# First-layer weights loaded by row blocks, six accumulators, and GpSimd normalizing the repeated rests: one change at the head of a fused attention and MLP kernel

## The chip, the cores and the metric

The kernel runs on one core of one Trainium2 chip. The metric is the device time of one execution in microseconds (us), median of several runs. Each number in a profile is from one profiled execution; its own device time stands beside its span below, since the span runs only from the first to the last instruction.

## The reference

For 2048 tokens of width 448, with xn the layer-normalized x:

```python
xn  = (x - mean(x)) / sqrt(var(x) + 1e-5)
q, k, v = split(xn @ wqkv, heads=16, width=28)
phi(t)  = where(t > 0, t + 1, exp(t)) + 1e-6
kv  = sum_s phi(k)[s] v[s]^T ;  z = sum_s phi(k)[s]
s   = (phi(q) @ kv / (phi(q) . z + 1e-6)) @ wo
h   = relu(xn @ w1 + b1) ** 2            # w1: 448 x 1792
g   = silu(h @ w2 + b2)                  # w2: 1792 x 448
out = x + s * g
```

All inputs and the output are bf16. Only the way from x and w1 to the first columns of h is touched by the change.

## The kernel before

**Tiles.** Tokens go in 16 tiles of 128 (index `si`), or in 4 groups of 512 (`g`). The contraction over 448 is cut into three chunks of 128 rows (c = 0, 1, 2) and a rest of 64 rows (c = 3). A rest would fill only half of TensorE's rows, so xn keeps its last 64 columns twice (columns 384 to 447 and again at 448 to 511), its transpose `xT` holds the rest in partitions 0 to 63 and again in 64 to 127, and two tiles' rests are run side by side in the two halves. The 1792 columns of h are 14 tiles (`fi`); `w_1` holds chunks 0 to 2, `w_1r` the rests.

**Order.** Every operation is recorded by `add` (L61) with its engine, the data it reads and writes and a guessed duration. `schedule` (L89) keeps PE (TensorE) and SP (the DMA issuing queue) in the order written, orders ACT (ScalarE), DVE (VectorE) and POOL (GpSimd) by readiness and due time, and hands out the eight PSUM banks. `emit` (L240) adds semaphore waits. At the head of the kernel `pr.hot` (L1202 to L1237) fixes the order on the three other engines as written, too.

**Loads at the head.** SP issues, in this order: x of token tiles 0, 1, 2 and 3 (L443 to L445); w1 in column blocks p of 512 columns (`load_w1`, L429): of p = 0 chunk 0 (128 KB), then chunks 1 and 2 (256 KB); of p = 1 all three chunks (384 KB) and two rest pieces of 32 KB; then x of tiles 4 to 7 (448 KB) and the k part of wqkv. ACT issues b1 and the two rest pieces of p = 0. Later, when the first transposed chunk of tokens 2 and 3 exists, SP issues w1 for p = 2 (384 KB and two rests), the q part of wqkv, then w1 for p = 3 (192 KB and two rests), and x of tiles 8 to 11. All issues are at L400.

**The first tokens.** For tiles 0 to 3: statistics on DVE (L463, L465), 1/std on ACT (L472, L476), xn on DVE (L483), the repeat of the rest by a copy (`dup`, L723: POOL for tiles 0, 1, 2, DVE for tile 3), transposes on PE (L743) and their copies from PSUM into `xT` (`evac`, L758 on DVE, L759 on ACT), one per chunk for tiles 0 and 1. Then h of group 0, in halves of 256 tokens: `pe_part` (L709) runs column tiles 0 to 3 for the first half chunk by chunk (12 matmuls), then tiles 4 and 5 with all three chunks (6 matmuls); 8 transposes of tiles 2 and 3; tile 6 (3 matmuls); the second half of tiles 0 to 3 (12 matmuls), their rests (L713, 4 matmuls), the second half of 4 to 6 (9), tile 7 (3), and the rests of 4 to 7 (4). Each finished column tile is relu'd (L680 on ACT, L685 on DVE) and squared (L694, L695), and its bank comes free.

**What follows.** Quads of k tiles and h tiles alternate (L1257). The first, K0.0 H0.8 K0.1 H0.10, needs the k weights, the p = 2 columns of w1 with both rests, and the banks of the first four column tiles (K0.0 and K0.1 those of tiles 0 and 2, H0.8 and H0.10 those of 1 and 3). Tokens from 512 on are transposed by DMA (L497), issued by SP behind the loads.

Of the kernel before, what the change touches and what calls it, by code (L numbers as in the profile page):

```python
# [6 lines left out]
ALU = mybir.AluOpType  # L7
AF = mybir.ActivationFunctionType

P = 128  # L10
S, D, F = 2048, 448, 1792
# [34 lines left out]
class Program:  # L46
# [14 lines left out]
    def add(self, eng, emit, reads=(), writes=(), dur=0.2, alts=(), nbytes=0):  # L61
        reads = [p for r in reads for p in self.aliases.get(r, (r,))]
        op = Op(eng, emit, reads, writes, dur, alts, nbytes)
        op.lead = self.lead
        if self.hot is not None:
            self.hot += 0.01
            op.prio = op.rank = self.hot
        for t in op.reads:
            w = self.writer.get(t)
            if w is not None:  # L70
                op.raw.add(w)
            self.readers.setdefault(t, []).append(op)
        for t in op.writes:
            w = self.writer.get(t)
            if w is not None and w is not op:
                op.deps.add(w)
            for r in self.readers.get(t, ()):
                if r is not op:
                    op.deps.add(r)
            self.writer[t] = op  # L80
            self.readers[t] = [r for r in self.readers.get(t, ()) if r is op]
        op.raw.discard(op)
        op.deps |= op.raw
        for d in op.deps:
            d.succ.append(op)
        self.ops.append(op)
        return op
# [212 lines left out]
def bass_recurrent_scan__linear_attn_block__dense_activation_squared_relu__prompt_kernel(  # L300
    nc, A_x, A_wqkv, A_wo, B_x, B_w1, B_b1, B_w2, B_b2, out
):
    with ExitStack() as es:
# [5 lines left out]
        ident = sb("ident", [P, P], bf)  # L309
# [5 lines left out]
        x_tok = sb("x_tok", [P, NT, D], bf)  # L315
        wqh = sb("wqh", [P, 64], bf)
        xn = sb("xn", [P, NT, 512], bf)
        xT = sb("xT", [P, NT, 4, P], bf)
        w_qkv = sb("w_qkv", [P, 4, 3 * D], bf)
        w_1 = sb("w_1", [P, 3, F], bf)  # L320
        w_1r = sb("w_1r", [P, 896], bf)
# [6 lines left out]
        mv = sb("mv", [P, NT, 2], f32)  # L328
        vep = sb("vep", [P, NT], f32)
        rstd = sb("rstd", [P, NT], f32)  # L330
# [68 lines left out]
        def dma(eng, dst, src, writes, nbytes, reads=(), dur=0.6):  # L399
            op = add(eng, lambda e, _: e.dma_start(dst, src), reads, writes, dur, nbytes=nbytes)  # L400
            if eng == "act":
                op.prio = -1000.0 + len(pr.ops)
# [4 lines left out]
        def load_w1r(p, eng2):  # L407
            lo, hi = 512 * p, min(512 * p + 512, F)
            m = (hi - lo) // 2
            for i in (0, 1):  # L410
                dma(
                    eng2, w_1r[64 * i : 64 * i + 64, 256 * p : 256 * p + m],
                    B_w1[384:448, lo + m * i : lo + m * i + m], [("w1", p, 1 + i)], 128 * m,
                )
# [11 lines left out]
        half_of = lambda fi: 1 if fi % 4 >= 2 or fi == 13 else 0  # L426
        rest_col = lambda fi: 768 if fi >= 12 else (fi // 4) * 256 + (fi % 2) * P

        def load_w1(p, eng, eng2, reads=()):  # L429
            lo, hi = 512 * p, min(512 * p + 512, F)  # L430
            m = (hi - lo) // 2
            for c0, c1 in ((0, 1), (1, 3)) if p == 0 else ((0, 3),):
                dma(
                    eng, w_1[:, c0:c1, lo:hi], B_w1[c0 * P : c1 * P, lo:hi].rearrange("(c p) j -> p c j", p=P),
                    [("w1", p, 0, c) for c in range(c0, c1)], (c1 - c0) * 256 * (hi - lo), reads,
                )
            load_w1r(p, eng2)

        w1names = lambda p: [("w1", p, i) for i in range(3)]
        for p in range(4):  # L440
# [3 lines left out]
        load_x(1, 2)  # L444
        load_x(2, 4)  # L445
        dma("act", b1r[:, :], B_b1.rearrange("(f p) -> f p", p=P), ["b1r"], F * 2)
        load_w1(0, "sp", "act")
        load_w1(1, "sp", "sp")
        load_x(4, 8)
        load_k("sp", w_qkv, A_wqkv, "wk", D, 2 * D)  # L450

# [15 lines left out]
        def ln_rstd(lo, hi):  # L467
            c = slice(lo, hi)
            ts = range(lo, hi)
            add(  # L470
                "act",
                lambda e, _: e.activation(out=vep[:, c], in_=mv[:, c, 1], func=AF.Ln, bias=eps5[:, 0:1]),  # L472
                [("mv", i) for i in ts] + ["eps5", "actw"], [("vep", i) for i in ts], 0.25,
            )
            add(
                "act", lambda e, _: e.activation(out=rstd[:, c], in_=vep[:, c], func=AF.Exp, scale=-0.5),  # L476
                [("vep", i) for i in ts], [("rstd", i) for i in ts], 0.2,
            )

        def ln_norm(si):  # L480
            add(
                "dve",
                lambda e, _: e.tensor_scalar(  # L483
                    out=xn[:, si, 0:D], in0=x_tok[:, si, :], scalar1=mv[:, si, 0:1],
                    scalar2=rstd[:, si : si + 1], op0=ALU.subtract, op1=ALU.mult,
                ),
                [("x", si), ("mv", si), ("rstd", si)], [("xn", si)], 0.36,
            )
# [81 lines left out]
        def pe_part(us, part, cs=(0, 1, 2)):  # L570
            def f(e, _):
                last = None
                for k in cs:
                    for u in us:
                        last = u[2](e, slice(0, 128), k, k == 0, False, part)
                return last

            need = {("xTp", 2 * part, k) for k in cs} | {u[1][0] + (k,) for u in us for k in cs}
            banks = [u[0] for u in us]
            add(  # L580
                "pe", f, sorted(need, key=str) + (banks if part or cs[0] else []), banks,
                len(us) * len(cs) * MM(256) + 0.01,
            )
# [134 lines left out]
            reads = xnames(g) if full else []  # L718
            return b, reads + w1names(fi // 4), mm, lambda: h_out(b, g, fi), 512

        def dup(lo, hi, eng="dve"):
            add(
                eng, lambda e, _: e.tensor_copy(xn[:, lo:hi, D:512], xn[:, lo:hi, 384:D]),  # L723
                [("xn", k) for k in range(lo, hi)], [("xnd", k) for k in range(lo, hi)], 0.25 if eng == "pool" else 0.18,
            )

        def x_transpose0(lo, pieces, share=()):
            bs = [None] * 4
            for p in pieces:
                b = Buf("T")  # L730
                for c in p:
                    bs[c] = b
            for c, o in share:
                bs[c] = bs[o]

            def piece(cs, ks=(0, 1)):
                def f(e, _):
                    last = None
                    for c in cs:
                        v = ps(bs[c])[:, :].bitcast(bf)  # L740
                        for k in ks:
                            o = (c * 2 + k) * P
                            last = e.transpose(v[:, o : o + P], xn[:, lo + k, c * P : (c + 1) * P], ident[:, :])  # L743
                    return last

                add(
                    "pe", f, [(("xnd" if 3 in cs else "xn"), lo + k) for k in ks] + ["ident"],
                    list(dict.fromkeys(bs[c] for c in cs)), len(cs) * len(ks) * 0.057,
                )

            def evac(eng, c0, c1):
                def f(e, _):
                    src = ps(bs[c0])[:, :].bitcast(bf)[:, c0 * 256 : c1 * 256].rearrange(
                        "p (c k t) -> p c k t", c=c1 - c0, k=2
                    )
                    dst = xT[:, lo : lo + 2, c0:c1, :].rearrange("p k c t -> p c k t")
                    if eng == "dve":
                        return e.tensor_copy(dst, src)  # L758
                    return e.activation(out=dst, in_=src, func=AF.Copy)  # L759

                du = 0.37 * (c1 - c0) if eng == "act" else 0.1 + 0.18 * (c1 - c0)
                return add(eng, f, [bs[c0]], [("xTp", lo, c) for c in range(c0, c1)], du)

            return piece, evac

        def bias_columns():
# [434 lines left out]
        H0 = {fi: hh(0, fi, fi >= 7) for fi in range(NF)}  # L1201
# [2 lines left out]
        ln_rstd(0, 1)  # L1204
        ln_stats(1)
        ln_norm(0)
        dup(0, 1, "pool")
        ln_rstd(1, 2)
        bias_columns()
        warm(4, 0.107)  # L1210
        ln_norm(1)
        dup(1, 2, "pool")
        ln_stats(2)
        piece, evac = x_transpose0(0, [(0,), (1,), (2,), (3,)])
        for c in range(4):
            piece((c,))
        evac("act", 0, 1)
        evac("act", 1, 2)
        ln_rstd(2, 3)
        evac("dve", 2, 3)  # L1220
        evac("act", 3, 4)
        ln_stats(3)
        ln_rstd(3, 4)
        ln_norm(2)
        dup(2, 3, "pool")
        ln_norm(3)
        dup(3, 4)
        for c in range(3):
            pe_part([H0[i] for i in range(4)], 0, (c,))
        pe_part([H0[i] for i in range(4, 6)], 0)  # L1230
        piece, evac = x_transpose0(2, [(0, 1, 2, 3)])
        piece((0, 1, 2, 3), (0,))
        piece((0, 1, 2, 3), (1,))
# [11 lines left out]
        pe_main(H0[7])  # L1245
        tails(H0[4], H0[6])
        last_tail = tails(H0[5], H0[7])
        load_w1(2, "sp", "sp", [("xTp", 2, 0)])
        load_k("sp", w_qkv, A_wqkv, "wq", 0, D)
        load_w1(3, "sp", "sp")  # L1250
        load_x(8, 12)
        ln(4, 8, lead=3, hold=[t23])
        z_masks([("xTp", 2, 3)])
# [94 lines left out]
```

## Time and profile before

| what | us |
|---|---|
| five runs, median (lowest to highest) | 144.6 (144.2 to 145.15) |
| the profiled execution, its own device time | 144.56 |
| its span, first to last instruction | 142.6 |
| outside the span | 1.96 |
| PE busy in the span | 137.6 (97%) |
| DVE, ACT, POOL busy | 93.7, 76.0, 32.7 |

In lists of the timeline the columns are: start, duration, engine, line, operation, out<-in, shape and count of neighbouring instructions merged into one row, and in brackets the idle time ahead with what ended it. PE is TensorE's matmul, PEld its weight load, SPq a DMA issue on SP. In the chain of work that ended last the columns are start, duration, what. TensorE's granted clock is full in every slice of this profile.

### The profile page before, as it was taken

What the parts mean: (1) busy time and instruction counts of PE and PEld (TensorE: products, weight loads), DVE (VectorE), ACT (ScalarE), POOL (GpSimd) and SP (SyncE); (2) the same over time, 40 slices, a digit from 0 to 9 for tenths busy, and PEclk for the clock granted to TensorE, in tenths of its full rate; (3) what the DMA queues carried; (4) which work ended last, traced back from release to release, by engine and by line L of the source; (5) the groups of instructions that cost most, each with busy time, mean ns of one, the idle gap of its engine ahead of it and who ended that gap; (6) DMA issues with size and microseconds to landing.
All of it is one profiled execution on the core that took longest, in us unless ns stands there. A gap on an engine that the chain in (4) does not pass through costs nothing.

```text
span 142.6 us, 2932 instructions
## 1 busy us (share of the span) xinstructions
PE 137.6 (97%) x1163; PEld 77.1 (54%) x1163; DVE 93.7 (66%) x217; ACT 76.0 (53%) x146; POOL 32.7 (23%) x49
## 2 busy tenths in 40 slices
PE   7789999999999999999999999999999999999991
PEld 7565555555566555555555455546555554554581
DVE  5849879799997556668997990004511882576582
ACT  3616798788876078888979781159322131100121
POOL 2105025145000107400660000000000000299900
PEclk9999999999999999999999999999999999999999
DMA  3887799990084300000002000000698000014332
GB/s 83 260 285 179 181 256 316 299 232 17 19 133 79 73 0 0 0 5 0 0 0 41 0 0 0 5 0 18 133 199 177 13 0 0 0 64 132 130 129 64
DMA packets 17568, 12.56 MB, mean 88 GB/s; under 512 B 8404, under 2 KB 16660, under 8 KB 17556
## 3 DMA queue, kind: packets, MB, share of 16 engines
q1 hardware_dynamic: 16976, 11.42, 30.8%
q10 hardware_dynamic: 580, 0.97, 3.2%
q8 instruction: 9, 0.15, 0.5%
q14 instruction: 3, 0.02, 0.1%
HBM read 8.78 MB, written 1.90 MB: 75 GB/s over the span
## 4 chain that ended last, share of the span: by engine, by line
PE 92%; DMA 4%; SPq 2%; DVE 1%; issue 0%; ACT 0%
PE pb L713 27%; PE pb L973 21%; PE pb L1008 7%; PE pb L621 7%; PE pb L782 6%; PE pb L647 6%; PE pb L1085 6%; DMA w<-in_B_w_dram 4%; PE pb L709 2%; PE pb L1032 2%; SPq L400 2%; PE pb L1158 1%; PE pb L661 1%; PE pb L788 1%; PE pb L861 1%; PE pb L810 1%
## 5 line engine op out<-in xcount | busy, mean ns | idle before, releaser
L713 PE MATMUL pb<-xT,w 64*128 64x512 bf16 (+1 forms) x291 | 38.7, 376 | 0.0
L680 ACT ACTIVATE r<-pb,b1f 128x512 bf16<-128x512 f32 x54 | 33.7, 692 | 7.3 <-PE pb L713 7.3
L973 PE MATMUL pb<-w,r 128*128 128x448 bf16 x154 | 30.0, 353 | 0.0
L713 PEld LDWEIGHTS pb<-xT,w 64*128 64x128 bf16 (+1 forms) x291 | 16.5, 94 | 14.3 <-ACT r L680 0.4
L1074 POOL TENSOR_TENSOR obuf<-obuf,x_tok 128x448 bf16<-128x448 bf16 x12 | 12.1, 1041 | 49.1 <-DVE obuf L1068 49.1
L1058 ACT ACTIVATE gbuf<-gbuf 128x448 bf16<-128x448 bf16 x15 | 8.1, 571 | 28.2 <-DVE gbuf L982 28.2
L973 PEld LDWEIGHTS pb<-w,r 128*128 128x128 bf16 x154 | 14.9, 98 | 14.1 <-DVE obuf L1068 0.4
L982 DVE TENSOR_TENSOR gbuf<-pb,b2b 128x448 bf16<-128x448 f32 x11 | 6.9, 623 | 23.6 <-PE pb L973 23.6
L694 DVE TENSOR_TENSOR r<-r 128x512 bf16<-128x512 bf16 x39 | 18.7, 518 | 2.1 <-ACT r L680 2.1
L631 POOL TENSOR_TENSOR zacc<-zacc,pk 128x448 f32<-128x448 f32 x13 | 14.4, 1106 | 22.7 <-DVE pk L611 19.3
L621 PE MATMUL pb<-w_qkv,xT 64*128 64x448 bf16 x112 | 13.4, 349 | 0.0
L599 ACT ACTIVATE pk<-pb 128x448 bf16<-128x448 f32 x16 | 7.8, 541 | 8.4 <-PE pb L621 8.4
L1068 DVE TENSOR_TENSOR obuf<-pb,gbuf 128x448 bf16<-128x448 f32 (+1 forms) x17 | 9.3, 591 | 3.2 <-PE pb L1085 2.4
L647 PE MATMUL pb<-xT,w_qkv 64*128 64x512 bf16 x84 | 11.2, 376 | 0.0
L1008 PE MATMUL pb<-w,r 64*128 64x448 bf16 x112 | 10.8, 349 | 0.0
L713 PE MATMUL pb<-xT,w_1r 64*128 64x512 bf16 x56 | 10.7, 377 | 0.0
L463 DVE BATCH_NORM_STATS2 st<-x_tok 128x6 f32<-128x448 bf16 x16 | 9.2, 614 | 1.6 <-DMA x_tok<-in_A_x_dram 1.6
L611 DVE SCALAR_TENSOR_TENSOR pk<-pb,pk 128x448 bf16<-128x448 f32 x16 | 9.9, 623 | 0.5
L695 ACT ACTIVATE r<-r 128x512 bf16<-128x512 bf16 x17 | 10.2, 634 | 0.0
L782 PE MATMUL pb<-pk,xn 128*128 128x448 bf16 x48 | 9.3, 353 | 0.0
L621 PEld LDWEIGHTS pb<-w_qkv,xT 64*128 64x128 bf16 x112 | 6.3, 94 | 5.1
L604 DVE TENSOR_SCALAR pk<-pk 128x448 bf16<-128x448 bf16 x16 | 6.2, 392 | 4.0 <-ACT pk L599 4.0
(90 smaller groups left out, 141.7 us busy)
## 6 DMA issues: line engine op xcount, KB each, us to landing
out_dram<-obuf SPq DMA_DIRECT2D x15, 112.0 KB, 1.7
w<-in_B_w_dram SPq DMA_DIRECT2D x1, 1568.0 KB, 9.8
x_tok<-in_A_x_dram SPq DMA_DIRECT2D x3, 448.0 KB, 4.5
w_qkv<-in_A_wqkv_dram SPq DMA_DIRECT2D x3, 336.0 KB, 5.8
w<-in_B_w_dram SPq DMA_DIRECT2D x2, 384.0 KB, 4.2
pk<-rden_rows ACTq DMA_DIRECT2D x6, 112.0 KB
pk<-rden_rows SPq DMA_DIRECT2D x5, 112.0 KB
w_o<-in_A_wo_dram SPq DMA_DIRECT2D x1, 392.0 KB, 10.1
```

What stands on the lines that cost most here:

```text
L611: lambda e, _: e.scalar_tensor_tensor(out=slot, in0=ps(buf)[:, 0:n], scalar=1.0 + 1e-6, in1=slot, op0=ALU.add, op1=ALU.max),
L621: return e.matmul(ps(b)[:, 0:D], xT[rw, si, c, :], w_qkv[rw, c, D : 2 * D], start=start, stop=stop)
L631: lambda e, _: e.tensor_tensor(out=o[:, 0:D], in0=pk[:, 0, :] if i == 1 else zacc[:, :], in1=pk[:, i, :], op=ALU.add),
L647: return e.matmul(ps(b)[:, 0:512], w_qkv[rw, c, m * P : (m + 1) * P], xT[rw, 4 * g : 4 * g + 4, c, :], start=start, stop=stop,)
L680: rl = lambda e, _: e.activation(out=slot, in_=ps(b)[:, 0:512], func=AF.Relu, bias=b1f[:, fi : fi + 1])
L694: return e.tensor_tensor(out=slot, in0=slot, in1=slot, op=ALU.mult)
L695: return e.activation(out=slot, in_=slot, func=AF.Square)
L713: return e.matmul(ps(b)[:, 0:512], lhs, xT[rw, 4 * g : 4 * g + 4, c, :], start=start, stop=stop, skip_group_check=not full,)
L782: last = e.matmul(ps(b)[:, 0:D], xn[:, si, c * P : (c + 1) * P], pk[:, si, :], start=(si == 0), stop=(si == NT - 1),)
L973: last = e.matmul(ps(b)[:, 0:D], r2[:, fi, si * P : (si + 1) * P], w_2[:, fi, :], start=(fi == 0), stop=(fi == NF - 1),)
L1008: last = e.matmul(ps(bufs[si])[:, 0:D], r2[half[h], fi, si * P : (si + 1) * P], w_2[half[h], fi, :], start=(i < 2 and fi == 0), stop=(i >= ...
L1074: lambda e, _: e.tensor_tensor(out=ob, in0=ob, in1=x_tok[:, si, lo:hi], op=ALU.add),
```

## The change

1. w1 for p = 0 and 1 is loaded together, by chunk: three DMAs of 128 rows by 1024 columns (256 KB each). The rests of both blocks go in two DMAs of 64 KB, on SP behind the chunks; ACT no longer issues any.
2. The first half of h of column tiles 0 to 5 is run chunk by chunk over all six accumulators (6 + 6 + 6 matmuls, where it was 12 for tiles 0 to 3 and then 6 for 4 and 5).
3. The repeated rests of tiles 0 to 3 are no longer copied from xn: POOL computes them from x with the same mean and 1/std (`norm_rest`).
4. Of the copies of tiles 0 and 1 into `xT`, chunk 1 goes from ACT to DVE and chunk 2 from DVE to ACT, and two of ACT's copies come after the 1/std of tiles 2 and 3.
5. The later load of w1 for p = 2 and p = 3 becomes one DMA of 128 x 3 x 768 (576 KB), followed by the rests of p = 2 and p = 3, all ahead of the q weights.

```diff
-        def load_w1(p, eng, eng2, reads=()):
-            lo, hi = 512 * p, min(512 * p + 512, F)
-            m = (hi - lo) // 2
-            for c0, c1 in ((0, 1), (1, 3)) if p == 0 else ((0, 3),):
+        def load_w1_rows(c0, c1, p0, p1, eng, reads=()):
+            lo, hi = 512 * p0, min(512 * p1, F)
+            dma(
+                eng, w_1[:, c0:c1, lo:hi], B_w1[c0 * P : c1 * P, lo:hi].rearrange("(c p) j -> p c j", p=P),
+                [("w1", p, 0, c) for p in range(p0, p1) for c in range(c0, c1)], (c1 - c0) * 256 * (hi - lo), reads,
+            )
+
+        def load_w1_rests(eng):
+            for i in (0, 1):
                 dma(
-                    eng, w_1[:, c0:c1, lo:hi], B_w1[c0 * P : c1 * P, lo:hi].rearrange("(c p) j -> p c j", p=P),
-                    [("w1", p, 0, c) for c in range(c0, c1)], (c1 - c0) * 256 * (hi - lo), reads,
+                    eng, w_1r[64 * i : 64 * i + 64, 0:512].rearrange("r (p j) -> r p j", p=2),
+                    B_w1[384:448, 0:1024].rearrange("r (p h j) -> r p h j", p=2, h=2)[:, :, i, :],
+                    [("w1", p, 1 + i) for p in (0, 1)], 64 * 1024,
                 )
-            load_w1r(p, eng2)
...
-        load_w1(0, "sp", "act")
-        load_w1(1, "sp", "sp")
+        for c in range(3):
+            load_w1_rows(c, c + 1, 0, 2, "sp")
+        load_w1_rests("sp")
...
-        def dup(lo, hi, eng="dve"):
-            add(
-                eng, lambda e, _: e.tensor_copy(xn[:, lo:hi, D:512], xn[:, lo:hi, 384:D]),
-                [("xn", k) for k in range(lo, hi)], [("xnd", k) for k in range(lo, hi)], 0.25 if eng == "pool" else 0.18,
+        def norm_rest(si):
+            add(
+                "pool",
+                lambda e, _: e.tensor_scalar(
+                    out=xn[:, si, D:512], in0=x_tok[:, si, 384:D], scalar1=mv[:, si, 0:1],
+                    scalar2=rstd[:, si : si + 1], op0=ALU.subtract, op1=ALU.mult,
+                ),
+                [("x", si), ("mv", si), ("rstd", si)], [("xnd", si)], 0.25,
             )
...
-        evac("act", 1, 2)
         ln_rstd(2, 3)
-        evac("dve", 2, 3)
-        evac("act", 3, 4)
+        evac("dve", 1, 2)
+        evac("act", 2, 3)
         ln_stats(3)
         ln_rstd(3, 4)
+        evac("act", 3, 4)
         ln_norm(2)
-        dup(2, 3, "pool")
+        norm_rest(2)
         ln_norm(3)
-        dup(3, 4)
-        for c in range(3):
-            pe_part([H0[i] for i in range(4)], 0, (c,))
-        pe_part([H0[i] for i in range(4, 6)], 0)
+        norm_rest(3)
+        first = [H0[i] for i in range(6)]
+        pe_part(first[0:4], 0, (0,))
+        pe_part(first[4:5], 0, (0,))
+        pe_part(first[5:6], 0, (0,))
+        pe_part(first, 0, (1,))
+        pe_part(first, 0, (2,))
...
-        load_w1(2, "sp", "sp", [("xTp", 2, 0)])
+        load_w1_rows(0, 3, 2, 4, "sp", [("xTp", 2, 0)])
+        load_w1r(2, "sp")
+        load_w1r(3, "sp")
         load_k("sp", w_qkv, A_wqkv, "wq", 0, D)
-        load_w1(3, "sp", "sp")
```

More of the change, by code (lines that the diff above doesn't have):

```diff
@@ L746, in piece @@
                 add(
-                    "pe", f, [(("xnd" if 3 in cs else "xn"), lo + k) for k in ks] + ["ident"],
+                    "pe", f, [(n, lo + k) for k in ks for n in (("xn", "xnd") if 3 in cs else ("xn",))] + ["ident"],
                     list(dict.fromkeys(bs[c] for c in cs)), len(cs) * len(ks) * 0.057,
@@ L1206, in bass_recurrent_scan__linear_attn_block__dense_activation_squared_relu__prompt_kernel @@
         ln_norm(0)
-        dup(0, 1, "pool")
+        norm_rest(0)
         ln_rstd(1, 2)
@@ L1211, in bass_recurrent_scan__linear_attn_block__dense_activation_squared_relu__prompt_kernel @@
         ln_norm(1)
-        dup(1, 2, "pool")
+        norm_rest(1)
         ln_stats(2)
```

## The prediction

> **What bounds the kernel now.** I read the busy shares first (PE 97%), then the chain of work that ended last, then the head of the timeline, the DMA issues with their landing times, and the DMA flow by stretch. The chain is 92% PE and, from 10.21 us to the end, PE back to back; so the time moves with the moment PE gets going, unless something later holds it. The chain's start, for 0 to 16 us (start, duration, what):
>
> ```profile
> 3.50 5.01 DMA w<-in_B_w_dram
> 8.51 0.05 issue
> 8.55 0.83 PE pb L709 x6
> 9.38 0.46 PE pb L743 x8
> ...
> 9.86 0.30 DVE xT L758
> ...
> 10.21 1.48 PE pb L709 x12
> ```
>
> The reader is to see that PE stood behind one transfer: the 384 KB of block p = 1, issued at 3.50 and landed at 8.51. PE's timeline gives the other hole:
>
> ```profile
> 6.34 0.61 PE L709 MATMUL pb<-xT,w 128*128 128x256 bf16 x4
> 7.46 1.92 PE L709 MATMUL pb<-xT,w 128*128 128x256 bf16 x14 [0.51 <-DMA w<-in_B_w_dram]
> ```
>
> Four matmuls of chunk 0, then a wait for chunks 1 and 2 of p = 0 (256 KB issued at 2.84 took 4.5 to land: 7.34). The matmuls start 0.11 apart, so 6.34 to 6.78, 7.46 to 8.34 and from 8.55 on is work; the first transpose of tiles 2 and 3 starts at 9.22, 0.67 after 8.55.
>
> A second place is easily missed: the first quad, where H0.8 needs w1 of p = 2, both its rests, and the banks of column tiles 1 and 3.
>
> ```profile
> 14.91 0.35 PE L621 MATMUL pb<-w_qkv,xT 64*128 64x448 bf16 x2
> 15.21 0.13 PEld L713 LDWEIGHTS pb<-xT,w 64*128 64x128 bf16 x3 [0.38 <-ACT r L680]
> ```
> ```profile
> 13.66 1.25 ACT L680 ACTIVATE r<-pb,b1f 128x512 bf16<-128x512 f32 x2
> ```
> ```profile
> w_1r<-in_B_w_dram SPq DMA_DIRECT2D x1, 32.0 KB, 4.0
> 11.15 0.60 SPq L400 DMA_DIRECT2D w_1r<-in_B_w_dram  x1
> ```
>
> The page names ACT, but those two relus end at 14.91. The second rest piece of p = 2, issued at 11.15 and 4.0 us under way, landed at 15.15: that is what released H0.8 (15.24). Without it PE, whose pairs start 0.19 apart, would have gone on at 15.10. So the head of the kernel has two gates, and a gain at the first counts only as far as the second lets it through.
>
> **The change, part by part.** All sums are against the profiled execution, 144.56 (span 142.6 and 1.96 around it); the median of the five runs is 144.6, 0.04 more.
>
> *Six accumulators by chunk.* Same 18 matmuls, no new ones. They now wait for three DMAs of 256 KB, issued in the same three slots of SP (2.20, 2.84, 3.50), in place of 128, 256 and 384 KB. The first group still starts at 6.34, when ACT's first copy ends (5.90 + 0.37). Landings, slow end: lay the new bytes on the old landings. Before, 640 KB (448 of x, 64 of rests on ACT, 128 of chunk 0) were down at 5.5, 896 at 7.34, 1280 at 8.51. Now chunk 0 ends at 704 KB: 5.5 + 64/256 x 1.84 = 5.96; chunk 1 at 960: 7.34 + 64/384 x 1.17 = 7.53; chunk 2 at 1216: 8.31. Then the third group starts at 8.35, the transposes at 9.02: 0.20 gained. Fast end: the flow in 3.0 to 5.5 us and in 24.0 to 24.5 us was
>
> ```profile
> DMA packets 581, 0.58 MB, mean 231 GB/s; under 512 B 66, under 2 KB 581, under 8 KB 581
> ```
> ```profile
> DMA packets 208, 0.19 MB, mean 373 GB/s; under 512 B 0, under 2 KB 208, under 8 KB 208
> ```
>
> so rows of 896 B (the second, w2) can flow at about 365; the head runs at 231 because the flow falters where new DMAs begin (74 GB/s in 3.0 to 3.25, 90 in 5.5 to 5.75). If that faltering goes, 992 KB after 3.0 need 2.8 us; with p = 1's own 1.26 from the end of flow (7.25) to landing, chunk 2 is down at 7.04, PE never waits, 6.34 + 18 x 0.11 = 8.32, xn of tile 3 is ready at 8.19: 0.90 gained. I take 8.0 for chunk 2, nearer the slow end because that is the row of this place: transposes at 8.71, **0.51 gained at the first gate**.
>
> *Rests of p = 0 from ACT to SP.* ACT idled there (to 3.84). SP issues five DMAs ahead of x of tiles 4 to 7 as before, so that one still goes out near 5.27. The rests are first needed at 11.63; cost nothing.
>
> *GpSimd's four normalizations.* No tensor_scalar on POOL is in the trace. Below: POOL's copy of the same 128x64 tile, 0.24. Above: its tensor_tensor on 448 columns, 1.04. At 0.24 they end before the copies they replace, since they wait for 1/std and not for xn. At 1.04 the second ends at 6.53, and the first group of h, queued behind its transpose on PE, starts near 6.75 and ends at 7.41, still ahead of chunk 1 at 7.53; with the early chunk 1 it would cost 0.4. I take zero, by the copy. DVE's copy of 0.18 at 8.23 goes, in a stretch where DVE idles until 9.86; worth nothing. The three copies on POOL never ran beside a normalization on DVE (385 ns mean); now the same 1/std releases both. The Trainium skill (SBUF — State Buffer, "Who interferes with whom") says that a tensor_scalar on VectorE in a two-port mode and a GpSimd instruction shut each other out for a whole instruction. By it xn of tile 1 would come 0.24 later and the first group of h at 6.58, which ends before chunk 1 of the slow end; the sum would be the same, and 0.24 worse only with chunk 1 early.
>
> *Copies into xT.* Chunk 1 moves to DVE (0.26 at 6.19), chunk 2 to ACT behind tile 2's 1/std: 6.80 to 7.17, ahead of its use; chunk 3 ends near 8.15, its bank is needed at 9.66. Nothing.
>
> *x of tiles 4 to 7.* Before it landed at 10.67, and DVE's four statistics began at 10.68, just as DVE's own copies ended. Next late: ACT's Ln at 13.22 waits for them, and the relus of column tiles 1 and 3 stand behind it. It can land unmoved (same bytes ahead) or up to 1.1 earlier (issue 5.27, and x of tile 0 needed 1.1 from issue to flow, against a flow that began at 7.5). In proportion to chunk 2 I take 10.4: ACT's relus end at 14.63.
>
> *The joint load of p = 2 and 3.* Issued after DVE's first copy, 10.18 - 0.51 = 9.67. The rests of p = 2 now stand behind 576 KB, not 384: 192 KB more, 0.54 at 365 GB/s, 0.85 at 231. I take 0.54, as it joins a running transfer (369 and 383 GB/s in 12.25 to 12.75). First rest: 13.8 - 0.51 + 0.54 = 13.83. The second landed 1.35 after the first; other pairs landed 0.13 (p = 1), 0.24 (p = 3) and 1.1 (p = 0) apart. I take 1.0, because with a longer load ahead both are queued when it ends: 14.83, H0.8 at 14.92. The four rests (2.3 us of issuing) now precede q's weights: those are issued 0.7 later, land near 17 and are needed at 20.15. x of tiles 8 to 11 and the DMA transposes gain, as SP has one issue of 0.6 less before them.
>
> **Sum.** H0.8 starts at the latest of PE 15.10 - 0.51 = 14.59, ACT 14.63 and the rest 14.92. Against 15.24: 0.32 less, 144.56 - 0.32 = **144.2**. After that PE had no stall longer than 0.1 that a shift could meet; PEld's other waits are hidden.
>
> **The rivals.**
> *Held at the second gate.* The rests lag by 1.35 again: 15.18, H0.8 at 15.27, 144.6. For it: same pair, same place. Also what comes out if p = 1's bytes were the limit and the first gate moves by 0.2 only.
> *Transfers without faltering.* Chunk 2 at 7.04, statistics 0.9 earlier, load issued at 9.28, rests by 13.6 to 14.4, H0.8 at 14.2 to 14.5: 143.5 to 143.8, say 143.65. For it: two fewer DMAs interleaved (ACT's flowed just in the first falter). Against: the second falter, at 5.5, had none of them.
> *The joint load lands late: slower.* First gate 0.20, the added 192 KB at 231 GB/s: 15.15 - 0.20 + 0.85 = 15.80, H0.8 at 15.89, 0.65 lost: 145.2. It decides as soon as the second rest lands after 15.15.
>
> **Chances.** Forecast 0.36, held 0.27, unfaltering 0.27, late load 0.10. Range 143.5 to 145.0, which leaves out the upper half of the last and some of the third. A measurement here tells about 0.5% (0.72 us) from no change: under 143.88 is most of the third case, 0.25; over 145.32 is the tail of the late load and of a slow GpSimd, 0.06; the rest 0.69.
>
> **What would show it.** Right: L709's third group of six starting near 8.0 with a DMA ahead of it; the first transpose of tiles 2 and 3 near 8.7; statistics of tiles 4 to 7 near 10.4; H0.8 near 14.9. Wrong: chunk 2 landing after 8.5; POOL's instruction over 1 us; H0.8's start unmoved although the transposes are earlier; PE stalls past 16 us that were not there.

## The result, and the profile after

The changed kernel takes **145.23 us** (median of 23 runs, 144.52 to 145.92) against 144.69 for the kernel before (42 runs, 144.20 to 145.15): ratio 1.0034, 95% interval 1.0022 to 1.0047. It is slower by about half a microsecond, where 144.2 was forecast; the time lies 0.2 above the range. The profiled execution took 145.33 with a span of 143.3 (before: 144.56 and 142.6).

In all that follows, **H0.8** is the first matmul that needs w1's third column block, and **the end** is the time from the end of DVE's last operation to the end of the span.

The page of the changed kernel, PE's share of the chain that ended last (92% before):

```profile
PE 88%; DMA 7%; SPq 2%; DVE 1%; issue 0%; ACT 0%
```

Transfers have 7% of the chain where they had 4%. The chain's head shows where (start, duration, what):

```profile
2.67 4.80 DMA w<-in_B_w_dram
7.47 0.05 issue
7.51 1.52 PE pb L715 x12
9.03 0.46 PE pb L753 x8
...
9.52 0.50 DVE xT L768 x2
10.02 0.20 SPq L400
10.22 0.04 issue
10.26 0.50 SPq L400
...
10.80 4.66 DMA w_1r<-in_B_w_dram
15.46 0.09 issue
15.55 1.04 PE pb L719 x8
```

Read it from the bottom. H0.8 (15.55) was released by the second rest piece of p = 2, issued at 10.80 and 4.66 under way. SP issued it behind the joint load, which waited for the first transposed chunk of tiles 2 and 3, which came behind the matmuls that waited for chunk 1 (landed at 7.47). PE's timeline has both gates in two rows:

```profile
7.51 1.52 PE L715 MATMUL pb<-xT,w 128*128 128x256 bf16 x12 [0.35 <-DMA w<-in_B_w_dram]
...
15.55 0.82 PE L719 MATMUL pb<-xT,w 64*128 64x512 bf16 x6 [0.64 <-DMA w_1r<-in_B_w_dram]
```

The first gate got better: chunk 2 is not waited for at all (12 matmuls in one row), and the transposes of tiles 2 and 3 start at 8.87 where they started at 9.22. The second got worse: PE now idles 0.64 there, and H0.8 starts at 15.55, 0.31 later than the 15.24 of before. From there on PE's rows are the old ones, all later by that 0.31 (the last 14 matmuls of g start at 138.36, before at 138.05).

Right behind the rests stood a second holder. DVE and ACT in the same stretch:

```profile
11.09 2.21 DVE L469 BATCH_NORM_STATS2 st<-x_tok 128x6 f32<-128x448 bf16 x4 [0.75 <-DMA x_tok<-in_A_x_dram]
...
14.05 1.25 ACT L686 ACTIVATE r<-pb,b1f 128x512 bf16<-128x512 f32 x2
```

x of tiles 4 to 7 landed at 11.05 in this execution (10.67 before), DVE waited 0.75 for it, so 1/std and the two relus behind it were late: 14.05 + 1.25 = 15.30 for the banks of column tiles 1 and 3.

The other part of the loss is where nobody computes. DVE's last row in the timeline, of the kernel before:

```profile
140.24 0.28 DVE L1074 TENSOR_TENSOR obuf<-obuf,x_tok 128x224 bf16<-128x224 bf16 x1
```

and of the changed kernel:

```profile
140.56 0.27 DVE L1084 TENSOR_TENSOR obuf<-obuf,x_tok 128x224 bf16<-128x224 bf16 x1
```

DVE's last operation ends at 140.52 and 140.83, 0.31 apart like everything since H0.8. The spans end at 142.6 and 143.3, 0.7 apart. So **the end takes 2.47 where it took 2.08** (spans are read to 0.1, so a value of the end is good to about 0.05), and the last store itself is no slower (1.5 from issue to landing in both). SP's own records show where the difference sits. L289 are the eight records of its last waits for output stores, L303 is the branch behind them (in these rows: shortest, median and longest duration in ns, then the first and last start in us). Before:

```profile
L289 SPq EVENT_SEMAPHORE  x8: 28/28/28, 140.9 to 142.1; - x8
L303 SPq COMPARE_BRANCH  x1: 38/38/38, 142.2 to 142.2; - x1
```

and after:

```profile
L289 SPq EVENT_SEMAPHORE  x8: 28/28/28, 141.2 to 142.4; - x8
L303 SPq COMPARE_BRANCH  x1: 38/38/38, 142.9 to 142.9; - x1
```

The branch starts 0.1 behind the start of the last wait in the kernel before and 0.5 behind it in the changed one; from the branch to the end of the span it is 0.4 in both. The sum of the loss: 0.31 at the second gate, 0.39 at the end, 0.07 outside the span, together the 0.77 between the two profiled executions.

### The profile page after: what moved, and what is told of

It reads as the page before. It is cut to its first block, busy times and chain, and to the rows that moved or that the text cites. A ratio compares the mean times of both kernels' runs of the same rounds, so it can differ in the third digit from the quotient of the medians.

```text
span 143.3 us, 2930 instructions
## 1 busy us (share of the span) xinstructions
PE 137.3 (96%) x1163; PEld 77.1 (54%) x1163; DVE 93.4 (65%) x216; ACT 76.3 (53%) x146; POOL 34.8 (24%) x50
## 4 chain that ended last, share of the span: by engine, by line
PE 88%; DMA 7%; SPq 2%; DVE 1%; issue 0%; ACT 0%
PE pb L719 25%; PE pb L983 20%; PE pb L1018 7%; PE pb L627 7%; PE pb L792 6%; PE pb L653 6%; PE pb L1095 6%; DMA w<-in_B_w_dram 3%; DMA w_1r<-in_B_w_dram 3%; PE pb L1042 2%; SPq L400 2%; PE pb L1168 1%; PE pb L667 1%; PE pb L715 1%; PE pb L798 1%; PE pb L871 1%
## 5 line engine op out<-in xcount | busy, mean ns | idle before, releaser
L719 PEld LDWEIGHTS pb<-xT,w 64*128 64x128 bf16 (+1 forms) x291 | 16.6, 94 | 14.8 <-ACT r L686 1.0
L983 PEld LDWEIGHTS pb<-w,r 128*128 128x128 bf16 x154 | 14.9, 98 | 14.1 <-DVE obuf L1078 0.4
L700 DVE TENSOR_TENSOR r<-r 128x512 bf16<-128x512 bf16 x39 | 17.8, 496 | 2.1 <-ACT r L686 2.1
L627 PE MATMUL pb<-w_qkv,xT 64*128 64x448 bf16 x112 | 13.5, 349 | 0.0
L1018 PEld LDWEIGHTS pb<-w,r 64*128 64x128 bf16 x112 | 6.4, 94 | 4.3
```

Source lines behind the costliest of these rows:

```text
L627: return e.matmul(ps(b)[:, 0:D], xT[rw, si, c, :], w_qkv[rw, c, D : 2 * D], start=start, stop=stop)
L700: return e.tensor_tensor(out=slot, in0=slot, in1=slot, op=ALU.mult)
L719: return e.matmul(ps(b)[:, 0:512], lhs, xT[rw, 4 * g : 4 * g + 4, c, :], start=start, stop=stop, skip_group_check=not full,)
L983: last = e.matmul(ps(b)[:, 0:D], r2[:, fi, si * P : (si + 1) * P], w_2[:, fi, :], start=(fi == 0), stop=(fi == NF - 1),)
L1018: last = e.matmul(ps(bufs[si])[:, 0:D], r2[half[h], fi, si * P : (si + 1) * P], w_2[half[h], fi, :], start=(i < 2 and fi == 0), stop=(i >= ...
```

## The experiments

All were run five rounds beside the kernel before on the same chip; times are medians, with H0.8 and the end from each one's profiled execution. Theory A: two things hold H0.8, the rests of p = 2 and the relus on ACT, so that both must go before it moves to where PE is ready (about 14.6 to 14.8). Rivals: the rests alone (B), the relus alone (C). Theory T, for the end: its length goes with the number of DMAs that SP issues. One row of H0.8 is one execution; the landings ahead of it differ from execution to execution.

| kernel | us, before beside it | ratio (95%) | H0.8 at, held by | SP's DMAs against after | end |
|---|---|---|---|---|---|
| before | 144.69 | | 15.24, rest | +1 | 2.08 |
| after | 145.23, 144.69 | 1.0034 (1.0022 to 1.0047) | 15.55, rest | 0 | 2.47 |
| later load split again | 144.48, 144.64 | 0.9983 (0.9969 to 0.9997) | 14.84, relus and rest | +1 | 2.07 |
| rests ahead | 144.72, 144.64 | 1.0004 (0.9987 to 1.0021) | 15.07, relus | 0 | 2.46 |
| relus first | 145.19, 144.64 | 1.0029 (1.0004 to 1.0055) | 15.57, rest | 0 | 2.44 |
| rests ahead, relus first | 144.49, 144.64 | 0.9990 (0.9976 to 1.0005) | 14.57, nothing | 0 | 2.46 |
| before, joint load alone | 145.16, 144.59 | 1.0047 (1.0030 to 1.0064) | 16.01, rest | 0 | 2.51 |
| after, wo in two | 144.88, 144.59 | 1.0017 (0.9999 to 1.0035) | 15.07, relus | +1 | 2.05 |
| later load split, copies back | 144.24, 144.59 | 0.9976 (0.9960 to 0.9991) | 14.91, nothing | +1 | 2.02 |
| rests ahead, relus first, wo in two | 144.10, 144.59 | 0.9968 (0.9955 to 0.9981) | 14.51, nothing | +1 | 2.02 |
| the same, copies back | 143.98, 144.51 | 0.9958 (0.9941 to 0.9974) | 14.52, nothing | +1 | 2.02 |
| before, one DMA less | 145.02, 144.51 | 1.0021 (0.9998 to 1.0044) | 15.32, rest | 0 | 2.49 |
| rests ahead, relus first, wo in three | 144.09, 144.51 | 0.9970 (0.9958 to 0.9982) | 14.80, nothing | +2 | 2.04 |

### The later load split again

```diff
-        load_w1_rows(0, 3, 2, 4, "sp", [("xTp", 2, 0)])
+        load_w1_rows(0, 3, 2, 3, "sp", [("xTp", 2, 0)])
         load_w1r(2, "sp")
-        load_w1r(3, "sp")
         load_k("sp", w_qkv, A_wqkv, "wq", 0, D)
+        load_w1_rows(0, 3, 3, 4, "sp")
+        load_w1r(3, "sp")
```

> The changed kernel with the joint later load undone: p = 2 with its rests, then q's weights, then p = 3. Theory A (two gates at the first quad: the rests of p = 2, which now queue behind 576 KB and landed at 15.46, and just behind them ACT's relus of column tiles 1 and 3, which ended at 15.30 because x of tiles 4 to 7 landed at 11.05): the second rest lands 0.5 earlier, near 14.9, and ACT then holds H0.8 at about 15.35, so 0.2 us less than the changed kernel, 145.0. Rival B (the load order is all of it): H0.8 at 14.9 and 0.6 less, 144.6.

144.48, ratio 0.9983: without the joint load the rest of the change is a small gain. The chain of this kernel:

```profile
5.06 5.46 DMA x_tok<-in_A_x_dram
...
13.60 1.16 ACT r L686 x2
14.76 0.08 issue
14.84 1.04 PE pb L719 x8
```

The chain names x of tiles 4 to 7 by way of the relus on ACT, which end at 14.76; but the second rest, issued at 10.62 and 4.1 under way, landed at the same moment (14.7 to 14.8), so this row doesn't tell which of the two held. In this execution x landed at 10.52, early for this order of loads (11.05 in after). The two numbers, H0.8 at 14.84 and 144.48, are those of rival B and not of theory A; but this kernel issues one DMA more and its end is 2.07, a cost that neither sum had, so the run by itself decides between them as little as its row does.

### The rests ahead

p = 2's two rests are issued behind the k weights, with no wait, and no longer behind the joint load.

```diff
         load_k("sp", w_qkv, A_wqkv, "wk", D, 2 * D)
+        load_w1r(2, "sp")
...
         load_w1_rows(0, 3, 2, 4, "sp", [("xTp", 2, 0)])
-        load_w1r(2, "sp")
         load_w1r(3, "sp")
```

> The changed kernel with the two rests of p = 2 issued early, right behind the k weights and without a wait, so that only the joint 576 KB load is still behind the wait. Theory A: the rests land before 13, H0.8 starts when ACT's relus end, 15.35: 0.2 us less than the changed kernel, 145.0. Rival B (the rests alone hold): H0.8 at 14.8, 0.75 less, 144.5. Rival C (x of tiles 4 to 7 and the chain behind it is the only gate, the rests only look late): no change or 0.1 less.

144.72, ratio 1.0004. The chain:

```profile
5.05 5.74 DMA x_tok<-in_A_x_dram
...
13.87 1.16 ACT r L687 x2
15.03 0.05 issue
15.07 1.04 PE pb L720 x8
```

With the rests out of the way H0.8 moves from 15.55 to 15.07 and stops there, on ACT. That refutes B (rests alone), which had PE going on as soon as it was ready; the median lies between the two forecasts, and the row decides. The move is larger than the 0.16 between the two holders in after (15.46 and 15.30), because x landed 0.26 earlier here (10.79).

### The relus first

ACT takes the relus of column tiles 1 and 3 ahead of the 1/std of tiles 4 to 7.

```diff
-        def ln_rstd(lo, hi):
+        def ln_rstd(lo, hi, hold=()):
...
+            ln_op.hold = hold
...
-            early = g == 0 and fi < 8
+            early = g == 0 and 4 <= fi < 8
...
-        ln(4, 8, lead=3, hold=[t23])
+        ln(4, 8, lead=3, hold=[t23], rhold=[relus[0, 1], relus[0, 3]])
```

> The changed kernel with ACT's order changed: the relus of column tiles 1 and 3 ahead of the 1/std of tiles 4 to 7 (which waits for late statistics); DVE takes the relu of tile 4 instead of 7 or 6. Theory A: the relus end near 14, but the rests still land at 15.46, so H0.8 stays at 15.55 and the time at 145.2. Rival C (statistics, 1/std, relu are the gate): H0.8 at 14.8, 144.5.

145.19, ratio 1.0029, as slow as the changed kernel. The chain:

```profile
10.77 4.71 DMA w_1r<-in_B_w_dram
15.48 0.09 issue
15.57 1.02 PE pb L722 x7
```

The four relus now end at 14.1, and H0.8 has not moved: the rest lands at 15.48. That refutes C.

### Both

> Both edits together, rests of p = 2 early and the relus ahead of the 1/std. Theory A: both gates are gone, H0.8 starts when PE gets there, 14.76, or when the joint load lands (14.04 in the changed kernel): 0.8 us less than the changed kernel, about 144.45, and 0.25 less than before. Rivals B and C expect no more than the better of the two single edits. If a third gate stands behind (DVE's relus, the bank of K0.2, k's weights), less than 0.8.

Both edits together: 144.49, ratio 0.9990. PE's timeline:

```profile
13.81 0.92 PE L629 MATMUL pb<-w_qkv,xT 64*128 64x448 bf16 x8
14.57 0.81 PE L723 MATMUL pb<-xT,w 64*128 64x512 bf16 x6
```

No bracket: H0.8 follows K0.0 without idle time, 0.98 earlier than in after. Either edit alone brought 0.48 and nothing, both bring the whole; theory A stands. But H0.8 is 0.67 earlier than in the kernel before, and this profiled execution only 0.2 shorter (144.35 to 144.56), because the end still takes 2.46.

### Before, with the joint load alone

The kernel before, with one DMA of 128 x 3 x 768 and the rests of p = 2 and p = 3 behind it, ahead of q's weights; everything else as it was.

```diff
-        load_w1(2, "sp", "sp", [("xTp", 2, 0)])
+        dma("sp", w_1[:, :, 1024:F], B_w1[0:384, 1024:F].rearrange("(c p) j -> p c j", p=P),
+            [("w1", p, 0, c) for p in (2, 3) for c in range(3)], 768 * (F - 1024), [("xTp", 2, 0)])
+        load_w1r(2, "sp")
+        load_w1r(3, "sp")
         load_k("sp", w_qkv, A_wqkv, "wq", 0, D)
-        load_w1(3, "sp", "sp")
```

> The kernel before with the joint load of p = 2 and 3 alone (576 KB, then four rests, then q's weights); nothing else changed. Theory A (gate): the first gate is unmoved, the second rest lands 0.5 later than 15.15, H0.8 starts near 15.75, 0.4 to 0.5 lost there. Theory T (a second cost at the end of the program: from the start of the last store to the end of the span the kernels with 46 rows in SP's program took 2.05, those with one SP DMA fewer 2.45): this kernel has one SP DMA fewer, so another 0.4: 145.4 in all. Rival (no cost at the end that belongs to SP's count): 145.05, and 2.05 at the end. Rival to A (p = 2's late landing came from the changed head alone): H0.8 unmoved at 15.24.

145.16, ratio 1.0047: this one edit costs as much as the whole change. From the chain of its profile:

```profile
14.11 1.74 ACT r L680 x3
15.85 0.16 issue
16.01 0.59 PE pb L713 x3
```

and the second rest of p = 2, its issue and its size and time to landing:

```profile
10.94 0.60 SPq L400 DMA_DIRECT2D w_1r<-in_B_w_dram  x1
w_1r<-in_B_w_dram SPq DMA_DIRECT2D x1, 32.0 KB, 5.0
```

The chain names a relu that ends at 15.85, but H0.8 starts 0.16 behind it, where it started 0.05 behind the relus when these held it (the rests ahead). The rest landed at 10.94 + 5.0 = 15.9, and H0.8 follows it by less than 0.1, as in before and after: the rest held it, 0.8 later than in the kernel before. So theory A's cost is in this profile, larger than the 0.4 to 0.5 forecast, and the end is 2.51, as theory T has it, with none of the change's edits at the first gate. The median lies between the 145.05 without a cost at the end and the 145.4 with it, and doesn't decide.

### One DMA more, where nothing waits for it

The changed kernel with the load of wo, first needed long after, cut in two.

```diff
-            dma("sp", w_o[0:PD, :, :], A_wo.rearrange("(c p) d -> p c d", p=PD), ["wo"], D * D * 2)
+            for i, (c0, c1) in enumerate([(0, 2), (2, 4)]):
+                dma("sp", w_o[0:PD, c0:c1, :], A_wo[c0 * PD : c1 * PD, :].rearrange("(c p) d -> p c d", p=PD),
+                    [("wo", i)], (c1 - c0) * PD * D * 2)
```

> The changed kernel with the load of wo, which is early by tens of us, cut into two DMAs of half its size, so that SP issues as many DMAs as e1. Theory T: H0.8 stays at 15.55, the end goes from 2.45 back to 2.05, 0.4 less: 144.85. Rival (the end depends on something else, or on chance): the end stays at 2.45 and the time at 145.2.

144.88, ratio 1.0017, the end 2.05. A DMA added makes the kernel shorter. In this profile H0.8 started at 15.07 and not at the 15.55 forecast, since the rests landed at 13.9 and 14.4 behind the same joint load (the reason stands under the joint load, below), so only the end of its row is evidence for T; the median, 0.0017 below after's ratio (0.25 us), is less than the 0.42 at the end but of its size, and the intervals overlap.

### The copies back

The later load split, and xn's rests copied as before in place of POOL's normalizations.

```diff
-        norm_rest(0)
+        dup(0, 1, "pool")
```

and so on for tiles 1, 2 (POOL) and 3 (DVE).

> e1 (changed head, later loads as before) with the copies of the rests back in place of GpSimd's normalizations. GpSimd's instruction took 0.63 to 0.79, not 0.24, but ends 0.2 before the transposes ask for it; if it costs nothing the time is e1's, 144.5 within 0.15. If its length or a shared port with DVE costs something at the first gate, 0.1 to 0.3 less than e1.

144.24, ratio 0.9976, against 0.9983 with the normalizations: not told apart.

### Both gates open, one DMA more

Rests ahead, relus first, and wo in two.

> e4 (rests of p = 2 early, relus ahead of the 1/std) with wo cut in two. Theories A and T together: no stall at H0.8 (14.6 to 14.8) and 2.05 at the end, 0.4 less than e4: 144.1, and 0.5 less than the kernel before. If T is wrong: 144.5 as e4.

144.10, ratio 0.9968 (0.9955 to 0.9981), the end 2.02. Against the same kernel with wo in one piece (0.9990) that is 0.0022, or 0.32 us, with H0.8 within 0.06. The chain from the last wait of PE on:

```profile
2.67 4.49 DMA w<-in_B_w_dram
7.16 0.04 issue
7.21 1.57 PE pb L724 x12
...
13.91 0.76 PE pb L634 x8
14.67 0.86 PE pb L728 x8
```

One transfer is left, chunk 1, and PE has nothing to wait for at the second gate. The spread went too: 143.86 to 144.34, where after had 144.52 to 145.92.

### The same with copies

> The version in which neither gate holds PE and SP issues one load more, with the repeated rests of tiles 0 to 3 copied from xn as in the kernel before (three on POOL, the fourth on DVE) in place of POOL's own normalizations. Theory (the normalizations lie off the path: POOL's 0.63 to 0.79 us end before the transposes that need them): no difference, 144.1, ratio 0.9968 within 0.001, H0.8 near 14.5. Rival (POOL's normalizations hold up DVE or POOL at the head, as the earlier pair of runs with 0.9983 and 0.9976 may hint): 0.1 to 0.2 us faster, 143.9 to 144.0, with chunk 1's matmuls or the transposes of tiles 2 and 3 earlier by as much.

143.98, ratio 0.9958 (0.9941 to 0.9974), the fastest of all. Against 0.9968 with POOL's normalizations the intervals overlap again; twelve matmuls, transposes and H0.8 are where they were (14.52, before 14.51). The time is the one that the rival named; its sign, matmuls or transposes earlier by 0.1 to 0.2, is not in the rows. Twice the copies came out 0.1 better, and neither time beyond the uncertainty: the normalizations are no gain, and a loss of 0.1 stays open.

### Before, with one DMA less

The two 16 KB rests of p = 3 in one DMA, at a place no wait of PE depends on.

```diff
+            if p == 3:
...
+                dma(
+                    eng2, w_1r[:, 256 * p : 256 * p + m],
+                    B_w1[384:448, lo:hi].rearrange("r (h j) -> h r j", h=2), [("w1", 3, "r")], 256 * m,
+                )
+                return
```

> The kernel before, with the two 16 KB rests of w1's last columns fetched by one DMA of 32 KB, so that SP issues one DMA less at a place that no wait of PE depends on. Theory (the longer end of the program hangs on how many DMAs SP issues in all): H0.8 unmoved near 15.2, but 2.45 us from the end of DVE's last operation to the end of the span where the kernel before has 2.05: 145.0, ratio 1.0028. Rival (the longer end belongs to the joint load or another part of the change, and only happens to go with the count): end 2.05, 144.6, ratio 1.000 within 0.001.

145.02, ratio 1.0021 (0.9998 to 1.0044). DVE's last row:

```profile
140.33 0.28 DVE L1082 TENSOR_TENSOR obuf<-obuf,x_tok 128x224 bf16<-128x224 bf16 x1
```

The span is 143.1: the end takes 2.49, where the kernel before has 2.08. H0.8 differs by 0.08 (15.32). So the longer end needs neither the joint load nor any other part of the change; one DMA fewer on SP brings it. The profile shows that plainly; the median by itself would not, its interval includes no change.

### Two DMAs more

Rests ahead, relus first, wo in three.

> The version with rests ahead and relus first, with the load of wo cut in three (2, 1 and 1 blocks of rows) where the fastest version has it in two: SP issues two DMAs more than the changed kernel, one more than the kernel before. If the end of the program is short from a certain count on: end 2.05, 144.1, ratio 0.9968. If it goes by steps with every DMA: end near 1.65, 143.7, ratio 0.994. If it alternates with the count: end 2.45, 144.5, ratio 0.999. H0.8 near 14.5 in each case.

144.09, ratio 0.9970, the end 2.04. It neither shortens with each DMA nor alternates: it is short from the count of the kernel before on, and long at one less, in all 13 profiles of the table. No kernel had still fewer. In all 13, too, the difference sits where it sat in before and after: SP's branch starts 0.04 to 0.07 behind the end of its last wait in the seven short ones, 0.45 to 0.47 in the six long ones. SP's records in the trace number 83 or 84 in the short ones and 82 in the long ones, so the runs don't tell the number of DMAs from the length of SP's program, which changed with it each time.

## Why the prediction was wrong, point by point

- **What bounds the kernel.** Right. Two gates at the head, where the kernels have a gate at all, and PE back to back after them in the chain of every kernel.
- **First gate.** 0.51 forecast, 0.35 measured in this profile: transposes at 8.87, not 8.71. It was worked out from the landing of chunk 2 alone (8.0, between the two ends). In fact chunk 2 was there when its turn came, and chunk 1 set the time: landed at 7.47, within 0.06 of the 7.53 of the slow end, and 12 matmuls of 0.11 behind it, 7.51 + 1.32 = 8.83. For 8.71, chunk 1 had to land by 8.71 - 1.32 - 0.04 = 7.35; the step did not ask for it. The size itself was fair: in the ten profiles with this head the transposes start between 8.52 and 8.94, with 8.71 in the middle.
- **POOL's normalizations.** They took 0.63 to 0.71, not the 0.24 of the copy, and cost nothing that these runs can tell, as forecast, since the last ended at 8.56, ahead of the transposes at 8.87. Rows of POOL in after:

```profile
4.47 1.42 POOL L730 TENSOR_SCALAR xn<-x_tok,mv,rstd 128x64 bf16<-128x64 bf16 x2 [2.90 <-ACT rstd L482]
6.93 0.63 POOL L730 TENSOR_SCALAR xn<-x_tok,mv,rstd 128x64 bf16<-128x64 bf16 x1 [1.05 <-ACT rstd L482]
7.86 0.70 POOL L730 TENSOR_SCALAR xn<-x_tok,mv,rstd 128x64 bf16<-128x64 bf16 x1 [0.29 <-ACT rstd L482]
```

DVE's four normalizations lasted 0.36, 0.40, 0.36 and 0.40, as before, so DVE paid nothing. The rule of the Trainium skill (SBUF — State Buffer, "Who interferes with whom") lets whichever instruction issues first shut the other out, when DVE's runs in a two-port mode. DVE delayed did not come true here, not even in the third pair, where POOL's began first (6.93, DVE's at 7.11). POOL delayed would fit the fourth pair in size, where DVE's began first (7.79, POOL's at 7.86): 0.24 + 0.40 = 0.64 against 0.70. But no run had POOL's instruction alone, and no view shows DVE's mode, so why it took that long stays open.

- **x of tiles 4 to 7.** Forecast at 10.4, landed at 11.05 in after, and between 10.5 and 11.1 in all ten profiles with this head; with the head of before it landed at 10.67, 11.03 and 10.0. So it was drawn forward in proportion to chunk 2 without a reason; nothing of that came, and the relus ended at 15.30, not 14.63. This alone would have put H0.8 at about 15.35, later than before.
- **The joint load: the step that failed first.** "The second landed 1.35 after the first ... I take 1.0, because with a longer load ahead both are queued when it ends: 14.83, H0.8 at 14.92." They were queued together, and landed 0.20 apart (10.26 + 5.0 = 15.26 and 10.80 + 4.66 = 15.46). But that brought the first rest back, not the second forward. Counted from the second rest of before: 15.15 - 0.35 + 0.66 = 15.46. The added 192 KB cost 0.66, between the two prices of 0.54 and 0.85; the miss of 0.63 is 0.35 from the shortened lag, 0.16 from the first gate and 0.12 from the bytes. The load's own part is steady: from issue to landing it took 4.0 to 4.6 in the nine kernels with 576 KB and 3.2 to 3.5 in the four with 384 KB.

The lag of the second rest behind its load is not steady: 1.53 in before, 1.46 in after, but 0.7 with wo in two, where the order of the loads up to the rests is the same. The flow behind the load doesn't explain it: it had the same hole in both. In after, and with wo in two:

```profile
13.50:14.25 0.75, 0.75 (x9) 0.37 (x10) 0.75 (x5) 0.61 (x3) 0.00 (x0) 1.00 0.44 55
13.50:14.25 0.75, 0.75 (x10) 0.38 (x8) 0.75 (x4) 0.72 (x3) 0.00 (x0) 1.00 0.40 50
```

The first two numbers of a row are the stretch and its length, the last two the DMA share and GB/s. What differs is a load of instructions. After, DMA queues in 12.0 to 13.5:

```profile
q8 instruction: 1, 0.02, 4.2%
```

This is one packet of 16 KB, and 4.2% of 16 engines over 1.5 us is one DMA engine for 1.0 us; the trace's packets have it from 13.11 to 14.12. Of the 128 rows of the two rests 120 had run by 13.75, and the last eight, one engine's sixteenth, ran one by one from 14.10 to 14.58. With wo in two that packet began at 16.16 and all 128 rows had run by 14.12. In the seven profiles where it began between 12.4 and 13.4, before and after among them, the second rest behind the load (of p = 2, or of p = 3 where those of p = 2 went ahead) landed 1.1 to 1.8 after it. Of the six where it began at 13.8 or later, five have 0.3 to 0.7; the sixth (later load split, copies back) has 1.45, which the packet doesn't explain. No run moved that packet, so this is read from traces and not shown by an experiment. A price per byte could not show it.

- **The end: not in the prediction.** "After that PE had no stall longer than 0.1 that a shift could meet" is true, and took for granted that what follows PE's last matmul stays as it is. It grew by 0.39, since the change issues one DMA less on SP. Of the 1.09 by which the profiled execution missed 144.24, 0.63 is the second gate, 0.39 the end, and 0.07 lies outside the span.
- **The rival that came.** "The joint load lands late: slower", at 0.10, priced 145.2. Its mechanism and its tipping point (a rest landing after 15.15) were right, its sum only by luck: it had 0.65 for the gate, and the profile has 0.31 there and 0.39 at the end. In the medians the share of the end is larger still: by its three tests, each with an interval of about 0.2 on either side or more, it is worth 0.25 (after against wo in two), 0.32 (both gates open, against wo in two) and 0.30 (before with one DMA less, 0.0021 x 144.5), of a loss of 0.0034 x 144.7 = 0.49. So the gate costs about 0.2 in the median, by difference, and varies from run to run with the landing of x and of the rests.
- **What it would have taken.** To see that both holders of H0.8 hang on transfers whose time of flight, 4 to 6 us, differed by up to one microsecond between executions with the same bytes ahead (x of tiles 4 to 7: 4.7 and 5.8 with the head of before; the second rest: 4.7 and 3.9 with the order of after), and to ask for each of them what comes if it lands no earlier. That gives H0.8 at 15.2 to 15.6, and no gain from the first gate.

What stays open: by what means one DMA fewer on SP puts 0.4 us between SP's last wait and its branch, and whether the DMA or the shorter program does it.

## What to carry to other kernels

A small transfer behind a bulk load lands later by the bulk's bytes, and in eight of these 13 profiles the second rest landed another 1.1 to 1.8 us behind the bulk itself, so what a later gate waits for should be issued ahead of a bulk load, not behind it (in the five kernels with the rests ahead they had landed by 12.9): moving two 32 KB rests and two relus turned a loss of 0.3% into no difference, and one DMA more into a gain of 0.3%. Where two holders end within 0.3 us of each other, removing one shows only the other: test them singly and together. And compare the stretch after the last computation too, since fewer DMA issues are not always a shorter program.

## What the runs showed of the hardware that was not expected

- The end of the program, 2.02 to 2.08 us in the seven kernels where SP issues at least as many DMAs as in the kernel before, 2.44 to 2.51 in the six where it issues one less; nothing between. The difference lies between SP's last wait and the branch behind it.
- In after the DMA flow was 77 GB/s in 10.25 to 11.75, 401 in 12 to 13 with the load of 576 KB (rows of 1536 B) under way, and 55 in 13.5 to 14.25 with DMAs of 32 KB pending.
- One 16 KB packet of instructions held one of the 16 DMA engines for 1.0 us (13.11 to 14.12 in after), and the last eight rows of two 32 KB DMAs ran as it ended (14.10 to 14.58).
- GpSimd's tensor_scalar with two scalars per partition on 128 x 64 took 0.63 to 0.71 beside DVE's normalizations, its copy of the same tile 0.24.
